# Attention and gated layer in one kernel: the two mask sizes read on one partition and spread by TensorE, fewer operations for the first masks, the later masks on GpSimd, and a new table of due dates

## The chip, the cores and the metric

One core of a Trainium2 chip runs the kernel. The metric is device time in microseconds (us). The kernel before takes 634.35 us, the median of 3 runs (634.06 to 634.65).

## The reference

Windowed attention with a few sink keys, followed by two dense layers with a gate between them. All inputs are float32; `n_sink` (4) and `window` (128) are two 64-bit integers that the kernel reads from memory while it runs.

```
q, k, v: (4, 8, 768, 64); w_in: (512, 2048); w_out: (2048, 512)
scores = (q @ k^T) / sqrt(64)
keep = (key < n_sink) | ((row - key >= 0) & (row - key < window))
a = softmax(where(keep, scores, -1e9)) / (sum + 1e-9)
x = (a @ v) as (3072, 512)
h = x @ w_in;  g = h - tanh(h);  out = g @ w_out
```

## The kernel before

**Work.** The 3072 rows are 12 chunks of 256 rows. Attention of a chunk is four units, one for each pair of heads. Unit u: its products (q times k, tile `s`) on TensorE, four merges on VectorE (add the mask, take the least, L727), four exponentials on ScalarE (L734), sums and reciprocals on VectorE (L742, L745), a scaling on GpSimd (L756) or ScalarE, transposes on TensorE (tile `t`), a copy on ScalarE (L766), and the products with the values (tile `x`). The dense layers of a chunk are eight groups of the hidden width: 24 matmuls `h` (L1023), a gate on ScalarE and VectorE, 12 matmuls `o` (L1075). The weights come as 64-bit words and are decoded on VectorE (L191 to L195).

**Order.** `Work.order` plans: every piece of work has an engine, a duration, a due date (which the table `PLAN` shifts) and its dependences. The planner takes the work in order of due dates as engines become free, and the result is each engine's program order. `BEGIN`, `COLD` and `came` are the planner's notions of when engines begin, until when TensorE is slow, and when the first keys and queries are there. Where the plan sees TensorE idle before its first dense step, `fill` puts in dummy matmuls of `ident` (tile `filled`, L1226). These are part of the program and run whether or not there is a gap.

**The start.** A first block stands ahead of the planned work: constants on GpSimd, the read of the sizes (`nswi`, L524) and of the first keys and queries, the masks of `_masks` on VectorE, and nine dummy matmuls (tile `warm`, L537). The two blocks are recorded separately and the framework puts them into one program per engine, so that an instruction of the second block can stand ahead of one of the first. Each engine runs its program in order.

**Masks.** The first chunks' units need `mask[:, 0]` (the diagonal block) and `wide` (two blocks side by side). Both depend on the sizes, which lie in `lim`. Three later closures (`merged`, `second`, `halves`, L159 to L175) make the masks of the later chunks and the row selectors `half` and `odd`, also on VectorE. The sizes reach all 128 partitions by one DMA that reads the same 16 bytes 128 times:

```
nc.scalar.dma_start(nswi, nsw.partition_broadcast(P))
```

The queries of units 0 and 1 follow it on ScalarE's DMA queue; unit 0's products need the queries and keys alone, the merges need products and masks. The products of units 0 and 2 share one pair of PSUM banks, those of 1 and 3 another, so that unit 2's products wait for unit 0's four merges.

Of the kernel before, what the change touches and what calls it, by code (L numbers as in the profile page):

```python
# [9 lines left out]
F32 = mybir.dt.float32  # L10
# [8 lines left out]
P = 128  # L19
# [4 lines left out]
NSK = 4  # L24
# [12 lines left out]
BIG = 3.0e38  # L37

# [4 lines left out]
    "first": -22200, "gate high": 12100, "gate low": -800, "gate tanh": 200, "second": -1800, "x high": -1700,  # L43
    "x low": 10100, ("attend", 0, 0): -2400, ("attend", 0, 2): 1300, ("attend", 2, 0): 1200, ("bits", 0): 26100,
# [3 lines left out]
    ("inverse", 1): 900, ("inverse", 2): -7600, ("late", 10, "values"): -7000, ("late", 11, "values"): 11500,  # L48
    ("late", 12): -5300, ("late", 13): -2400, ("late", 14): -200, ("late", 15): 8600, ("late", 16): -4400,
    ("late", 17): -2000, ("late", 18): 3600, ("late", 19): 1800, ("late", 20): -900, ("late", 22): -500,  # L50
    ("late", 23): -200, ("late", 24): 300, ("late", 25): 2900, ("late", 27): 2700, ("late", 28): -1900,
    ("late", 29): 3200, ("late", 30): 18900, ("late", 31): 500, ("late", 32): -8700, ("late", 34): 12800,
    ("late", 35): -2700, ("late", 36): -2000, ("late", 37): -2000, ("late", 38): -1200, ("late", 4, "values"): -8200,
    ("late", 40): -7200, ("late", 41): 100, ("late", 42): 12300, ("late", 43): -6000, ("late", 44): -500,
    ("late", 45): -11100, ("late", 46): 100, ("late", 47): 3800, ("late", 5, "values"): 1900,
    ("late", 6, "values"): 200, ("late", 7, "values"): -2200, ("late", 8, "values"): -4000,
    ("late", 9, "values"): 600, ("load", 10): -100, ("load", 2): -2100, ("load", 3): 3200, ("load", 4): -3200,
    ("load", 5): -500, ("load", 6): -200, ("load", 7): 8000, ("load", 8): 400, ("masks", 0): 5600,
    ("masks", 1): -2600, ("merge0", 0): 8900, ("merge0", 1): 5000, ("merge0", 2): -500, ("merge1", 0): 2600,
    ("merge1", 1): -3800, ("products", 0): 9800, ("products", 1): 1200, ("products", 2): -6300, ("scale0", 2): -500,  # L60
    ("step", 0): 18000, ("step", 1): 20100, ("step", 11): -1600, ("step", 12): 2900, ("step", 13): 100,
    ("step", 16): 3800, ("step", 17): -3300, ("step", 18): 600, ("step", 19): -700, ("step", 20): -300,
    ("step", 21): 600, ("step", 23): -3600, ("step", 25): -700, ("step", 26): -3400, ("step", 27): -1300,
    ("step", 28): 600, ("step", 29): -1600, ("step", 3): 100, ("step", 30): 2800, ("step", 32): -4500,
    ("step", 33): 600, ("step", 34): 500, ("step", 35): -4000, ("step", 36): -6600, ("step", 37): 100,
    ("step", 38): 4900, ("step", 39): 1200, ("step", 4): 800, ("step", 40): 5200, ("step", 41): -1200,
    ("step", 42): -5100, ("step", 43): 2900, ("step", 44): -1900, ("step", 45): 4400, ("step", 46): -3200,
    ("step", 47): -3300, ("step", 48): -1900, ("step", 49): 1000, ("step", 5): -900, ("step", 50): 3400,
    ("step", 51): 1200, ("step", 52): -1200, ("step", 53): -2300, ("step", 54): 6900, ("step", 57): -2900,
    ("step", 58): -2400, ("step", 59): -200, ("step", 6): 2800, ("step", 60): -6700, ("step", 61): -4300,  # L70
    ("step", 62): -200, ("step", 63): 700, ("step", 64): 500, ("step", 65): 7400, ("step", 66): 7000,
    ("step", 67): -1300, ("step", 69): -6600, ("step", 7): 900, ("step", 71): 1300, ("step", 72): 5100,
    ("step", 73): -100, ("step", 75): 2100, ("step", 76): -7500, ("step", 77): 400, ("step", 78): -13200,
    ("step", 79): 300, ("step", 8): -300, ("step", 80): -5700, ("step", 81): 1100, ("step", 84): 1600,
    ("step", 85): 1000, ("step", 86): -2400, ("step", 88): 1800, ("step", 9): -2000, ("step", 90): 14900,
    ("step", 91): -200, ("step", 92): 1000, ("step", 93): 3400, ("step", 94): 800, ("step", 95): -2000,
    ("sums", 0): -1000, ("sums", 1): -5200, ("sums", 2): -2200, ("transposes0", 0): 3600, ("transposes0", 1): -400,
    ("transposes0", 2): -3200, ("unit", 0): -100, ("unit", 1): 10700, ("unit", 10): -3200, ("unit", 11): 900,
    ("unit", 2): -1700, ("unit", 4): -3200, ("unit", 5): 1300, ("unit", 6): -8400, ("unit", 7): 1200,
    ("unit", 8): -2500, ("unit", 9): 4700, ("value in", 0): 2500, ("value in", 1): -1400, ("values", 0): 300,  # L80
    ("values", 1): -4700, ("values", 2): 7300, ("values", 3): 1400, ("values in", 1): -800, ("values in", 2): -4500,
    ("weights", 0, 0): -1800, ("weights", 0, 1): 1700, ("weights", 0, 2): 7300, ("weights", 0, 3): 11300,
    ("weights", 0, 4): 400, ("weights", 0, 5): 3700, ("weights", 0, 6): 700, ("weights", 0, 7): 8800,
    ("weights", 1, 0): 100, ("weights", 1, 2): -100, ("weights", 1, 3): -500, ("weights", 1, 4): 100,
    ("weights", 1, 5): -3900, ("words", 0, 0): 300, ("words", 0, 1): -5100, ("words", 0, 2): -100,
    ("words", 0, 3): -2200, ("words", 0, 5): 700, ("words", 0, 6): -200, ("words", 0, 7): 9400,
    ("words", 1, 0): 17700, ("words", 1, 1): 5500, ("words", 1, 2): 2100, ("words", 1, 3): 1300,
    ("words", 1, 4): 2700, ("words", 1, 5): -900, ("words", 1, 6): 700, ("words", 1, 7): 7400,
# [3 lines left out]
SCALES = (("POOL", "POOL", "ACT"), ("POOL", "POOL", "ACT"))  # L92
# [3 lines left out]
def kernel(  # L96
# [16 lines left out]
    nswi = cpool.tile([P, 4], I32, tag="nswi", name="nswi")  # L113

    pts = cpool.tile([P, NPAIR, 2, 4, P], F32, tag="pt", name="pt")
    et = mybir.EngineType
    bad = _banded(tc, cpool, qd, kp, vp, vs, nsw, nswi, w_in, w_out, ident, pts, out)


    with tc.If(bad != 0, preferred_fallthrough_block=True, label="rare"):  # L120
        _general(tc, qd, kp, vp, nswi, w_in, w_out, ident, xd, out)
# [1330 lines left out]
```

## Time and profile before

| | us |
|---|---|
| median of 3 runs | 634.35 |
| the profiled execution | 634.26 |
| its span on the engines | 632.5 |
| TensorE busy | 626.3 |
| VectorE busy | 365.7 |
| ScalarE busy | 303.7 |
| GpSimd busy | 51.5 |

The profiled execution lies within the three runs, and 1.8 us of it are outside the span. Busy time of TensorE holds its dummy matmuls too (`warm` and `filled`), so that a busy TensorE at the start need not be one that gets on. PE is TensorE's matmuls, PEld its weight loads, DVE VectorE, ACT ScalarE, POOL GpSimd; a q behind a name is the engine's queue of DMA issues. A float32 matmul shows as two records.

### The profile page before, as it was taken

To read this page: it belongs to the slowest core of one execution; us is meant where nothing else is said; L and a number is where in the kernel's file an instruction comes from. 1 tells how busy PE (TensorE), PEld (TensorE's weight loads), DVE (VectorE), ACT (ScalarE), POOL (GpSimd) and SP (SyncE) were. 2 spreads that over 40 slices of the span, in tenths; PEclk is the share of its full clock that TensorE was granted. 3 is DMA by queue.
4 is the path that set the end of the run, shared out by engine and by line. 5 is a ranking of instruction groups with operands and counts; after the bars stand their busy time and mean duration, and the time that the engine had idled before them with its cause. 6 is when DMAs were issued, how large, how long until landed. Compare 5 with 4: busy or idle time off the path is not lost.

```text
span 632.5 us, 14875 instructions
## 1 busy us (share of the span) xinstructions
PE 626.3 (99%) x5796; PEld 562.7 (89%) x5796; DVE 365.7 (58%) x1038; ACT 303.7 (48%) x851; POOL 51.5 (8%) x153
## 2 busy tenths in 40 slices
PE   9999999999999999999999999999999999999997
PEld 7788899989899899899989989999989899899995
DVE  8999999627556665346451655556562456632221
ACT  6857654337365464345352626547352445522222
POOL 4711010001000000000000000000000000000000
PEclk9999999999999999999999999999999999999999
DMA  8986242014343253133240125235332134210001
GB/s 259 365 345 205 89 139 66 1 67 136 105 160 106 72 169 118 32 117 113 61 148 34 52 77 175 78 80 172 106 97 72 51 85 137 96 30 2 33 1 37
DMA packets 70156, 67.81 MB, mean 107 GB/s; under 512 B 20929, under 2 KB 57537, under 8 KB 70081
## 3 DMA queue, kind: packets, MB, share of 16 engines
q1 hardware_dynamic: 69648, 66.55, 33.0%
q8 instruction: 47, 0.77, 0.5%
q10 hardware_dynamic: 432, 0.26, 0.2%
q14 instruction: 29, 0.23, 0.1%
HBM read 49.87 MB, written 16.91 MB: 106 GB/s over the span
## 4 chain that ended last, share of the span: by engine, by line
PE 99%; ACT 0%; issue 0%; DVE 0%; DVEq 0%; ACTq 0%
PE h L1023 42%; PE o L1075 42%; PE x L950 4%; PE s L620 3%; PE x L810 1%; PE t L762 1%; PE filled L1226 1%; PE s L716 1%; PE s_x L620 1%; PE warm L537 1%; PE x L938 1%; PE s_t L716 1%; ACT w L995 0%; ACT pt L766 0%; PE s_t L620 0%
## 5 line engine op out<-in xcount | busy, mean ns | idle before, releaser
L1023 PE MATMUL h<-xh,w 128*128 128x256 f32 x1536 | 277.9, 278 | 0.0
L1023 PEld LDWEIGHTS h<-xh,w 128*128 128x128 f32 x1536 | 237.6, 188 | 4.3 <-issue 1.2
L1023 PE MATMUL h<-xl,w 128*128 128x256 f32 x768 | 212.4, 277 | 0.0
L1075 PE MATMUL o<-w,gh 128*128 128x512 f32 x768 | 193.8, 392 | 0.0
L1075 PEld LDWEIGHTS o<-w,gh 128*128 128x128 f32 x768 | 139.2, 188 | 27.2 <-issue 0.8
L1031 DVE TENSOR_TENSOR h<-h,graw 128x512 f32<-128x512 f32 x96 | 66.8, 696 | 158.2 <-ACT graw L1028 157.7
L1023 PEld LDWEIGHTS h<-xl,w 128*128 128x128 f32 x768 | 144.3, 188 | 2.3
L1028 ACT ACTIVATE graw<-h 128x512 f32<-128x512 f32 x96 | 57.1, 595 | 161.2 <-PE h L1023 160.4
L1075 PE MATMUL o<-w,gl 128*128 128x512 f32 x384 | 103.5, 390 | 0.0
L1035 ACT CAST gh<-h 128x512 fp32r<-128x512 f32 x96 | 56.1, 585 | 64.6 <-DVE h L1031 49.8
L1039 DVE TENSOR_TENSOR gl<-h,gh 128x512 fp32r<-128x512 f32 x96 | 65.8, 686 | 35.3 <-ACT gh L1035 31.7
L1075 PEld LDWEIGHTS o<-w,gl 128*128 128x128 f32 x384 | 71.4, 188 | 14.8 <-issue 0.3
L648 ACT ACTIVATE p<-p,st 128x132 f32<-128x132 f32 x144 | 56.8, 397 | 31.4 <-DVE st L640 30.1
L672 ACT ACTIVATE p<-p,st 128x132 f32<-128x132 f32 x144 | 46.2, 397 | 4.2 <-DVE st L667 3.7
L864 DVE STREAM_TRANSPOSE pt<-p 128x512 f32<-128x512 f32 x36 | 25.5, 709 | 25.0 <-ACT p L672 25.0
L677 POOL CAST z<-p 128x16 fp32r<-128x16 f32 x36 | 7.1, 197 | 379.4 <-ACT p L672 305.1
L635 DVE COPY_PREDICATED s<-ident,s 128x256 f32<-128x256 uint32 x49 | 20.8, 425 | 15.7 <-PE s L620 15.2
L640 DVE CUSTOM_DVE_ANT_0 p<-s,mask 128x132 f32<-128x132 f32 x104 | 26.6, 293 | 2.6
L648 ACT ACTIVATION_READ_ACCUMULATOR p<-p,st 128x1 f32 x144 | 27.2, 189 | 0.0
L620 PEld LDWEIGHTS s<-kraw,qraw 64*64 64x64 f32 x832 | 21.8, 132 | 5.1 <-issue 3.9
L950 PE MATMUL x<-pt,v 64*64 64x192 f32 (+2 forms) x832 | 25.2, 271 | 0.0
L620 PE MATMUL s<-kraw,qraw 64*64 64x64 f32 (+3 forms) x832 | 24.6, 251 | 0.2 <-PE x L950 0.2
(109 smaller groups left out, 498.2 us busy)
## 6 DMA issues: line engine op xcount, KB each, us to landing
turned<-pt SPq DMA_DIRECT2D x36, 256.0 KB, 2.1
pt<-turned SPq DMA_DIRECT2D x144, 64.0 KB, 2.0
wraw<-w_in SPq DMA_DIRECT2D x16, 512.0 KB, 6.1
wraw<-w_out SPq DMA_DIRECT2D x16, 512.0 KB, 6.9
kraw<-kp SPq DMA_DIRECT2D x36, 196.0 KB, 3.1
out<-ob SPq DMA_DIRECT2D x24, 256.0 KB, 2.2
v<-vp SPq DMA_DIRECT2D x42, 128.0 KB, 2.9
qraw<-qd SPq DMA_DIRECT2D x40, 128.0 KB, 2.5
```

The source lines that it names most:

```text
L620: nc.tensor.matmul(y, lhsT=qt[u][HALF[h], t * P + half * Q : t * P + half * Q + Q], rhs=k, start=True, stop=True,)
L640: nc.vector.tensor_tensor_reduce(out=pr[u][:, j, :], in0=where[0][h][:, TS * t : TS * t + TS], in1=mask[:, kind, :], scale=-0.125, scalar= ...
L648: nc.scalar.activation(e, e, AF.Exp, bias=st[u][:, j : j + 1], scale=-1.0, accum_out=st[u][:, 4 + j : 5 + j],)
L672: nc.scalar.activation(pr[u][:, j, :], pr[u][:, j, :], AF.Copy, scale=s[:, 8 + j : 9 + j])
L864: nc.vector.transpose(dst, pr[u][:, :, NSK:].rearrange("p n (b j) -> p n b j", j=32))
L950: nc.tensor.matmul(xps[key][r][h * 64 : h * 64 + 64, j, a:z], lhsT=vt[cc, i][HALF[r], y, hd : hd + D], rhs=weight_columns(j, y, blk)[HALF[ ...
L1023: nc.tensor.matmul(y, lhsT=w, rhs=x, start=r == 0, stop=r == 11)
L1028: nc.scalar.activation(gr[n], hps[n], AF.Tanh)
L1031: nc.vector.tensor_tensor(hps[n], hps[n], gr[n], op=ALU.subtract)
L1035: nc.scalar.copy(gh[n], hps[n])
L1039: nc.vector.tensor_tensor(gl[n], hps[n], gh[n].bitcast(F32), op=ALU.subtract)
L1075: nc.tensor.matmul(y, lhsT=(gh, gh, gl)[i][n][:, f, t * P : (t + 1) * P], rhs=w, start=first and not low and r == 0, stop=bool(last and lo ...
```

## The change

The sizes are read once, into one partition (`one`). VectorE converts them to two floats, TensorE multiplies them with a row of ones (`ones`), which spreads them over 128 partitions, and VectorE copies the result into `lim`. The function `got`, which does this, is called in the middle of `_masks`. Instead of nine dummy matmuls there are four before and three after it. After the sizes are known VectorE does four mask operations on 128x128 ahead of the first merge; before it did six, with six of the later masks' operations between them. The masks of the later chunks and the selectors go to GpSimd (two bit operations stay on VectorE). All due dates and some of the planner's constants are new; one scaling of the third chunk goes from ScalarE to GpSimd; the piecewise first matmul of a block (`H_PIECES`, `O_PIECES`), there before after some kinds of work, is now used after `<lambda>` too (the early transposes and value products) and is of another form after `values`. `_general`, which does not run with these sizes, reads the sizes for itself.

```diff
-    "first": -22200, "gate high": 12100, "gate low": -800, "gate tanh": 200, "second": -1800, "x high": -1700,
+    "first": -700, "gate difference": -14100, "gate high": -1200, "gate low": -700, "gate tanh": -200,
...
-SCALES = (("POOL", "POOL", "ACT"), ("POOL", "POOL", "ACT"))
+SCALES = (("POOL", "POOL", "POOL"), ("POOL", "POOL", "ACT"))
...
+    back = mask[:, 1, NSK:]
+    nc.gpsimd.memset(mask[:, 0, :NSK], NEG)
 
     def halves():
         for pair, bit in ((half, 16), (odd, 32)):
             part = scr[:, 3, bit : bit + 1].bitcast(I32)
             nc.vector.tensor_scalar(part, rows, bit, None, op0=ALU.bitwise_and)
-            nc.vector.tensor_copy(pair[:, 0:1], part)
-            nc.vector.tensor_scalar(pair[:, 1:2], pair[:, 0:1], 1.0, None, op0=ALU.is_ge)
-            nc.vector.tensor_scalar(pair[:, 0:1], pair[:, 0:1], 1.0, None, op0=ALU.is_lt)
+            nc.gpsimd.tensor_copy(pair[:, 0:1], part)
+            nc.gpsimd.tensor_scalar(pair[:, 1:2], pair[:, 0:1], 1.0, None, op0=ALU.is_ge)
+            nc.gpsimd.tensor_scalar(pair[:, 0:1], pair[:, 0:1], 1.0, None, op0=ALU.is_lt)
...
+    nc.vector.scalar_tensor_tensor(wide[:, 1, :], above, FAR, diff, op0=ALU.mult, op1=ALU.add)
+    nc.vector.tensor_scalar(wide[:, 0, :], diff, 0.0, FAR, op0=ALU.is_ge, op1=ALU.mult)
+    nc.vector.scalar_tensor_tensor(wide[:, 0, :], wide[:, 0, :], float(P), diff, op0=ALU.add, op1=ALU.add)
+    got(lim, halves)
+    n_sink, window = lim[:, 0:1], lim[:, 1:2]
+    nc.vector.tensor_scalar(col, col, n_sink, NEG, op0=ALU.is_ge, op1=ALU.mult)
+    nc.vector.scalar_tensor_tensor(mask[:, 0, NSK:], wide[:, 1, :], window, col, op0=ALU.is_ge, op1=ALU.mult)
+    nc.vector.scalar_tensor_tensor(wide[:, 0, :], wide[:, 0, :], window, col, op0=ALU.is_ge, op1=ALU.mult)
+    nc.vector.tensor_scalar(wide[:, 1, :], wide[:, 1, :], window, NEG, op0=ALU.is_ge, op1=ALU.mult)
+    on = nc.gpsimd
+    on.tensor_scalar(below, diff, 0.0, None, op0=ALU.is_le)
...
+    on.tensor_tensor(mask[:, 1, :NSK], tmp[:, :NSK], col[:, :NSK], op=ALU.add)
...
-    BEGIN = {"PE": 5000.0, "ACT": 3600.0, "DVE": 5300.0, "POOL": 3000.0, "SP": 1700.0}
+    BEGIN = {"PE": 4600.0, "ACT": 3600.0, "DVE": 4900.0, "POOL": 8000.0, "SP": 1700.0}
...
-            nc.scalar.dma_start(nswi, nsw.partition_broadcast(P))
+            nc.scalar.dma_start(one[:, :4], nsw)
...
+            def got(lim, meanwhile):
+                two = one[:, 4:6].bitcast(F32)
+                nc.vector.tensor_copy(two, one[:, 0:4].rearrange("o (v w) -> o v w", w=2)[:, :, 0])
+                meanwhile()
+                nc.tensor.matmul(warm[:, 1, 1, 0:2], lhsT=ones, rhs=two, start=True, stop=True)
+                nc.vector.tensor_copy(lim, warm[:, 1, 1, 0:2])
...
+            keep_warm(4)
+            mask, above, below, after, half, odd = _masks(nc, outer, got, scr, wide)
+            keep_warm(3)
...
-            for _ in range(9):
-                nc.tensor.matmul(warm, lhsT=hot, rhs=hot, start=True, stop=True)
```

TensorE's program at its start, before. `s_191`, `s_202`, `s_229` and `s_247` are the products of units 0 to 3, `t_0_277` and `t_1_292` the transposes of unit 0.

```order
L537 MATMUL warm<-pt 128x128 x9
L716 MATMUL s_191<-lent_6_121 128x128 x2
L716 MATMUL s_191<-lent_6_121 128x256 x2
L716 MATMUL s_202<-lent_6_121 128x128 x2
L716 MATMUL s_202<-lent_6_121 128x256 x2
L1226 MATMUL filled<-ident 128x128 x5
L716 MATMUL s_229<-lent_6_121 128x128 x2
L716 MATMUL s_229<-lent_6_121 128x256 x2
L716 MATMUL s_247<-lent_6_122 128x128 x2
L716 MATMUL s_247<-lent_6_122 128x256 x2
L1226 MATMUL filled<-ident 128x128 x7
L762 MATMUL t_0_277<-ident,lent_7_124 128x128 x2
```

The same place now, where `s_207`, `s_215` and `s_249` are the products of units 0 to 2 and L545 is the matmul that spreads the sizes:

```order
L550 MATMUL warm<-pt 128x128 x4
L732 MATMUL s_207<-lent_6_120 128x128 x2
L732 MATMUL s_207<-lent_6_120 128x256 x2
L732 MATMUL s_215<-lent_6_120 128x128 x2
L732 MATMUL s_215<-lent_6_120 128x256 x2
L1242 MATMUL filled<-ident 128x128 x4
L545 MATMUL warm<-one,ones 128x2
L1242 MATMUL filled<-ident 128x128 x2
L550 MATMUL warm<-pt 128x128 x3
L1242 MATMUL filled<-ident 128x128
L732 MATMUL s_249<-lent_6_120 128x128 x2
L732 MATMUL s_249<-lent_6_120 128x256 x2
```

L545 was recorded ahead of all of the planned work, and in the program it stands behind the products of units 0 and 1 and four dummies. In all there were 28 `filled` and 9 `warm` before, and there are 27 and 7 now; behind unit 0's first transposes stand 20 of the `filled` now, where 16 stood before.

VectorE's program ahead of the first merge, before, from the mask operation that follows the sizes' two conversions to the first merge (L727); `lent_7_124` holds `wide` among others, `lent_7_125` the scratch:

```order
L152 TENSOR_SCALAR lent_7_125<-lent_7_125,few 128x128
L153 TENSOR_TENSOR lent_7_124<-mask,lent_7_125 128x128 [waits DVE_49]
L161 COPY mask<-lent_7_125 128x4 [waits DVE_49]
L162 TENSOR_SCALAR lent_7_125<-mask,few 128x128
L154 TENSOR_TENSOR mask<-lent_7_124,lent_7_125 128x128 [waits DVE_49]
L155 TENSOR_TENSOR lent_7_124<-lent_7_124,mask 128x128
L165 COPY mask<-mask 128x128 [waits DVE_49]
L156 TENSOR_TENSOR lent_7_124<-lent_7_124,lent_7_125 128x128 [waits DVE_49]
L166 TENSOR_TENSOR lent_7_125<-lent_7_125 128x128
L167 TENSOR_TENSOR mask<-lent_7_125 128x4 [waits DVE_49]
L727 ISA lent_7_124<-s_191,mask 128x128 [waits PE_49,Pool_49]
```

The same place now, where L543 converts the two sizes, L546 copies what TensorE spread, and L743 is the first merge:

```order
L543 CAST one<-one 1x2 [waits DMAHW0_49]
L149 TENSOR_SCALAR lent_7_124<-lent_7_124 128x1 [waits Pool_49]
L149 TENSOR_SCALAR lent_7_124<-lent_7_124 128x1
L546 COPY few<-warm 128x2 [waits PE_49]
L162 TENSOR_SCALAR lent_7_124<-lent_7_124,few 128x128 [waits DVE_49]
L165 SCALAR_TENSOR_TENSOR mask<-lent_7_123,few,lent_7_124 128x128 [waits DVE_49]
L166 SCALAR_TENSOR_TENSOR lent_7_123<-lent_7_123,few,lent_7_124 128x128
L167 TENSOR_SCALAR lent_7_123<-lent_7_123,few 128x128 [waits DVE_49]
L743 ISA lent_7_123<-s_207,mask 128x128 [waits Pool_49]
```

The chain from the sizes to the first merge is shorter on VectorE, and it now goes through TensorE's program by way of the wait of L546.

## Rows read from the trace of the kernel before

**Rows 1.** The page's busy times: busy us, share of the span, instructions.

```profile
PE 626.3 (99%) x5796; PEld 562.7 (89%) x5796; DVE 365.7 (58%) x1038; ACT 303.7 (48%) x851; POOL 51.5 (8%) x153
```

**Rows 2.** Stretches of the span: length, busy us by engine, granted clock, DMA share, GB/s.

```profile
2.00:4.00 2.00, 2.00 (x11) 2.00 (x11) 0.82 (x3) 1.28 (x1) 0.91 (x6) 1.00 0.52 98
4.00:6.00 2.00, 2.00 (x15) 1.59 (x13) 1.57 (x11) 0.00 (x0) 0.23 (x1) 1.00 1.06 364
10.00:25.00 15.00, 15.00 (x135) 12.31 (x134) 14.72 (x59) 13.22 (x49) 11.62 (x10) 1.00 1.00 357
25.00:50.00 25.00, 24.82 (x188) 20.92 (x187) 24.76 (x48) 17.41 (x44) 6.77 (x6) 1.00 0.87 335
```

**Rows 3.** Waits of TensorE in the whole span: total, times, longest.

```profile
PE s L620 <- PE x L950: 0.2, 1, 0.2
PE x L810 <- ACT pt L766: 0.2, 1, 0.2
```

**Rows 4.** Timeline of TensorE's first 12 us: start, duration, [idle before].

```profile
1.15 3.92 PEld L537 LDWEIGHTS warm<-pt 128*128 128x128 f32 x18 [1.15 <-DVE pt L520]
5.29 1.69 PE L716 MATMUL s<-lent 64*128 64x128 f32 x16
6.03 0.55 PEld L716 LDWEIGHTS s<-lent 64*128 64x128 f32 x8 [0.21 <-issue]
6.91 1.19 PEld L1226 LDWEIGHTS filled<-ident 128*128 128x128 f32 x10 [0.33 <-issue]
8.22 1.81 PE L716 MATMUL s<-lent 64*128 64x128 f32 x16
9.97 1.64 PEld L1226 LDWEIGHTS filled<-ident 128*128 128x128 f32 x14 [0.33 <-issue]
11.63 0.38 PE L762 MATMUL t<-ident,lent 128*128 128x128 f32 x2
```

**Rows 5.** All of the tile `filled`: records, min/median/max ns, first and last start.

```profile
L1226 PE MATMUL filled<-ident x56: 275/275/377, 6.9 to 25.0; 128*128 128x128 f32 x56
```

**Rows 6.** DMA issues of the first 12 us: KB each, us from issue to landing.

```profile
lent<-qd ACTq DMA_DIRECT2D x2, 128.0 KB, 4.0
nswi<-nsw ACTq DMA_DIRECT2D x1, 2.0 KB, 3.6
```

**Rows 7.** The page's DMA issues of the whole span, queries.

```profile
qraw<-qd SPq DMA_DIRECT2D x40, 128.0 KB, 2.5
```

**Rows 8.** Timeline of all engines' first 11 us, ScalarE's DMA issue and VectorE.

```profile
1.26 0.93 ACTq L127 DMA_DIRECT2D lent<-qd  x2
4.43 0.15 DVE L148 CAST few<-nswi 128x1 f32<-128x1 int32 x1 [1.61 <-DMA nswi<-nsw]
4.70 0.28 DVE L151 TENSOR_SCALAR mask<-mask,few 128x128 f32<-128x128 f32 x1
4.89 0.28 DVE L152 TENSOR_SCALAR lent<-lent,few 128x128 f32<-128x128 f32 x1
6.75 0.29 DVE L727 CUSTOM_DVE_ANT_0 lent<-s,mask 128x128 f32<-128x128 f32 x1
7.86 0.29 DVE L727 CUSTOM_DVE_ANT_0 lent<-s,mask 128x128 f32<-128x128 f32 x1
8.97 0.15 DVE L172 TENSOR_SCALAR lent<-lent 128x1 int32<-128x1 int32 x1
10.23 0.15 DVE L742 TENSOR_REDUCE lent<-lent 128x4 f32<-128x8 f32 x1
```

**Rows 9.** The same timeline, ScalarE's exponentials and GpSimd's first scaling.

```profile
7.08 0.40 ACT L734 ACTIVATE lent<-lent 128x128 f32<-128x128 f32 x1 [3.58 <-DVE lent L727]
8.85 0.49 ACT L734 ACTIVATE lent<-lent 128x256 f32<-128x256 f32 x1
10.77 3.18 POOL L756 TENSOR_TENSOR lent<-lent 128x256 f32<-128x256 f32 x4 [5.70 <-DVE lent L727]
```

**Rows 10.** The chain that ended last, in order of time: start, duration, blocks of 48.

```profile
79.50 5.65 PE h L1023 x48
94.66 5.45 PE h L1023 x48
```

More of the change, by code (lines that the diff above doesn't have):

```diff
@@ L51 @@
[L51 to L65, printed above, removed]
@@ L76 @@
[L76 to L80, printed above, removed]
@@ L86 @@
[L86 to L88 removed]
+    "first": -700, "gate difference": -14100, "gate high": -1200, "gate low": -700, "gate tanh": -200,
+    "second": 33200, "weights low": -2000, "x high": 3000, ("attend", 0, 0): -7100, ("attend", 0, 2): -1400,
@@ new lines @@
+    ("load", 4): 3200, ("load", 5): -9200, ("load", 6): 900, ("load", 7): 400, ("load", 8): -200, ("load", 9): -100,
+    ("masks", 0): 800, ("masks", 2): 2600, ("merge0", 0): -6100, ("merge0", 1): -300, ("merge0", 2): 12400,
+    ("merge1", 0): 1700, ("merge1", 2): -12000, ("products", 0): 7600, ("products", 1): -2500, ("products", 2): 3300,
+    ("scale0", 0): -26200, ("scale0", 1): -4100, ("scale0", 2): 1200, ("scale1", 0): -3200, ("scale1", 2): -800,
+    ("step", 0): -600, ("step", 1): -1300, ("step", 10): -7200, ("step", 11): 5100, ("step", 12): -3400,
@@ L527, in _banded, with keep_warm @@
                 _load_pair(nc.scalar, qt[u], qd[0, 2 * u : 2 * u + 2, :, :CH])
-                work.came.update({r: (5050.0, 5300.0)[u] for r in slots(u)})
+                work.came.update({r: (4600.0, 4900.0)[u] for r in slots(u)})
             make_identity(nc, ident)
-            mask, above, below, after, rest, half, odd = _masks(nc, outer, nswi, scr, wide)
             nc.gpsimd.memset(stats, 1e-9)
-            nc.gpsimd.memset(mask[:, 0, :NSK], NEG)
+            def got(lim, meanwhile):
[4 more added lines that the diff above has]
+                nc.vector.tensor_copy(lim, warm[:, 1, 1, 0:2])
+            def keep_warm(n):
+                for _ in range(n):
+                    nc.tensor.matmul(warm[:, 0, 0, :], lhsT=hot, rhs=hot, start=True, stop=True)
+            keep_warm(4)
+            mask, above, below, after, half, odd = _masks(nc, outer, got, scr, wide)
+            keep_warm(3)
             nc.gpsimd.memset(zt.bitcast(F32), 0.0)
             nc.gpsimd.memset(vsink.bitcast(F32), 0.0)
-            warm = ps_t.tile([P, 2, 2, P], F32, tag="t", name="warm")[:, 0, 0, :]
-            for _ in range(9):
-                nc.tensor.matmul(warm, lhsT=hot, rhs=hot, start=True, stop=True)
-        for i, part in enumerate(rest):
-            work.add("DVE", (650, 600, 1320)[i], 45000, part, (), ["mask", "scratch"], tags=(("masks", i),))
         def corners():
@@ L1246, in _rare, with _general @@
     return bad
-def _general(tc, qd, kp, vp, nswi, w_in, w_out, ident, xd, out):
+def _general(tc, qd, kp, vp, nsw, w_in, w_out, ident, xd, out):
     nc = tc.nc
```

116 lines of the change are left out of this document (63 added, 53 removed), and 6 rows, old and new, of the table PLAN.

## The prediction

> **What bounds the kernel now.** I read the busy times first, then the stretches, then TensorE's waits, then the first 12 us row by row. TensorE is busy for 626.3 of 632.5 us [rows 1], and apart from its beginning it waits for two things, 0.2 us each [rows 3]. So the dense part is a stream of matmuls with no holes, and time can be won or lost in two ways only: in what TensorE does that nobody needs, and in how even the stream is. The unneeded part lies in the first 25 us: 1.15 us before its first instruction, nine `warm` matmuls up to about 5.1 us, and 28 `filled` (56 records) from 6.9 to 25.0 us [rows 4, 5]. A `filled` costs 1.19 / 5 = 0.24 us [rows 4], so all of them 6.7 us. They hide a second bound. From 10 to 25 us VectorE is busy for 14.72 of 15 us, and from 25 to 50 us for 24.76 of 25 [rows 2]: the start goes at the pace of VectorE, and TensorE's dummies lie in its gaps.
>
> What starts VectorE's real work is the first merge at 6.75 us [rows 8]. The sizes land at 4.43 us; some 2.3 us of mask work follow. Unit 0's products start at 5.29 us [rows 4], right behind the landing of its queries (issue at 1.26 us and 4.0 us of flight give 5.26) [rows 6, 8], and are done before the masks. So the masks hold the first merge by a little, and the queries stand close behind.
>
> **The change, part by part.** The order of TensorE's program decides. The matmul that spreads the sizes stands behind the products of units 0 and 1 and four `filled`; every mask that VectorE still has to make, and so every merge, waits for it. Queued behind L546 on VectorE is everything it does; ScalarE waits for the merges, GpSimd and TensorE for ScalarE. I follow this chain and then add up TensorE's time.
>
> *Start of unit 0's products.* The 128 small reads are gone from the queue ahead of the queries. While they ran DMA moved 98 GB/s from 2 to 4 us, and 364 GB/s from 4 to 6 us, after they had landed [rows 2, 6]. The best that the queries could do is the flight of later ones, 2.5 us [rows 7]: 1.26 + 2.5 = 3.8 us. The worst is no change, 5.3 us. I take 4.7 us, a little above the middle, since keys and queries of two units still share the engines: **-0.6 us**.
>
> *TensorE's clock.* Before, 18 records of `warm` take 3.92 us, 218 ns each, and the same shape as `filled` takes 119 ns [rows 4]. That is the slow level (1.2 GHz) against the fast one (2.4 GHz), though the column of the granted clock says 1.00 for both [rows 2]; I go by the pace. The fast pace came after 3.9 us without a pause. Now four `warm` end at 1.15 + 8 x 0.218 = 2.9 us, and TensorE stands still until 4.7. Unit 0's products took 6.03 - 5.29 = 0.74 us [rows 4]; at the slow pace 0.74 x 218 / 119 = 1.36. I take one unit at the slow pace, **+0.6 us**. The bounds are none (0) and all until the sizes are spread (below).
>
> The Trainium skill, "TensorE: Matmul & The Clock Gate", Part 1: The HAM clock gate, says that the array's clock is throttled by default and that sustained activity releases it. The first rows agree in direction (218 ns, then 119); no row shows what a pause does. By that rule the shorter run of `warm` does not count and the slow pace lasts longer; that is the first rival.
>
> *To the first merge.* Unit 0: 4.7 to 6.1. Unit 1, with the gap behind it, 6.91 - 6.03 = 0.88 us [rows 4]: 7.0. Four `filled`: 7.9. L545 has no row; it costs between nothing and a lone transpose (0.38 us, [rows 4]). I take 0.3, since the weight load is the same however few columns follow: 8.2. Then VectorE: a hand-over of 0.1 (the exponential at 7.08 follows a merge of 0.29 begun at 6.75 by less than that [rows 8, 9]), the copy, and four mask operations at 0.2 to 0.25 us (4.70 to 4.89 is one step, [rows 8]; three-operand ones are unknown, hence the upper value), 1.2 us in all. The first merge is at 9.4 us, 2.65 us later than before, although the work behind the sizes shrank from 2.3 to 1.2 us.
>
> *From there to the transposes of unit 0.* Unit 0's merges take 7.86 - 6.75 = 1.1 us [rows 8], so unit 2's products can start at 10.6. TensorE, having done three `filled` and three `warm` (6 x 0.24), is there at 9.6: **idle 1.0**. Unit 3's wait for unit 1's merges, at 9.4 + 2.2 = 11.6 [rows 8]; products of two units take 9.97 - 8.22 = 1.75 us [rows 4], so **idle 0.2**, done at 12.5. Four exponentials take 1.8 us from 0.33 us behind the first merge [rows 8, 9]; with their tail and the second unit's merges VectorE comes to unit 0's sums at 11.7. Before it came to them at 10.23, 1.26 us after its last merge, because eight one-column operations of `halves` stood in between [rows 8]; these leave, and are worth 1.26 us on this chain. From the sums to the scaling are 0.54 us, and from there to the transposes 0.86 [rows 4, 8, 9]: 13.1 us, **idle 0.6**. Before: 11.63.
>
> *TensorE's sum.* Start -0.6, clock +0.6, L545 +0.3, three `warm` at the fast pace +0.7, one `filled` less -0.2, idle 1.0 + 0.2 + 0.6 = +1.8: +2.6 us. As a test, by the transposes: 13.1 - 11.63 = 1.5, and four more `filled` behind them 0.95 give 2.4. A lost microsecond can't be made good later, since the stream behind has no holes [rows 3].
>
> *The dense part.* A block of 48 `h` took 5.45 us, or 5.65 when it ran unevenly [rows 10]; the new pieces after early transposes and value products can spare some 0.1 us for 24 matmuls at four to seven places. I take **-0.4 us** (0 to -0.8).
>
> *Hidden.* GpSimd's masks: it stood idle for 5.7 us before its first scaling at 10.77 [rows 9], and the six operations behind the sizes, at some 0.3 us (a scaling takes 3.18 / 4 = 0.8 us on two to four times the columns), end near 11.5 us, before the scaling at 12.2. Without that cover each microsecond more delays the transposes as much. The moved scaling of the third chunk lies where ScalarE and GpSimd have room (17.41 and 6.77 of 25 us, [rows 2]). `_general` does not run.
>
> Together +2.2 us. The profiled execution took 634.26 us, 0.1 under the median, so 636.5 us.
>
> **The rivals.** *The clock stays low until the sizes are spread.* For it: a pause of nearly 2 us that was not there. Against: `warm` still runs 1.7 us. Unit 1 costs 0.55 x 99 / 119 = 0.5 us more, four `filled` 4 x 0.2 = 0.8, L545 0.2: +1.5 us, 638.0 us.
>
> *The queries land at 3.8 us and the clock is fast for them.* The whole chain moves by 0.9 + 0.6 us: +0.7, 635.0 us. For it: the low DMA rate beside the small reads. Against: it needs both best cases.
>
> *TensorE doesn't hold up the sizes, and the kernel is faster.* If the spread is there by the time unit 0's products end (6.1 us), the first merge comes at about 6.3 us. The transposes then come at 6.3 + 3.7 = 10.0 instead of 11.63; with four more `filled` and the pieces -1.6 + 0.95 - 0.4 = -1.1, 633.2 us. It decides whether L545 executes before 5 us. For it: VectorE's 1.26 us saved on a stage that it bounds. Against: the place in the program, behind matmuls that wait for queries.
>
> **How the numbers follow.** Forecast 0.57 (635.5 to 637.4), low clock 0.16, early queries 0.16, faster 0.11. A change under 0.2% (1.3 us) is about what a measurement of this kernel can't tell from none, so slower is above 635.6: the forecast without its lowest part, and the low clock, 0.70. Same: the early queries and that lowest part, 0.19. Faster 0.11. The range of 8 in 10 leaves out the faster case and the far end where late queries (+0.6) and a low clock meet: 634.2 to 638.6.
>
> **What would show it.** First merge between 9 and 10 us, right behind L546, which waits for TensorE; L545 after 8 us; TensorE idle for about 1 us before unit 2's products; no new waits after 25 us. If L545 stands before 5 us or the first merge before 7, the step on the order is wrong; if the pace of unit 0's products is fast, the step on the clock; if GpSimd's masks end after 12.2 us, they are not hidden; if TensorE waits in the dense part, the due dates matter, which I counted at nothing.

## The result, and the profile after

The changed kernel takes 638.8 us (median of 4 runs, 638.4 to 639.6) against 634.5 us, a ratio of 1.007 with an interval of 1.0052 to 1.0087. It is slower by 4.3 us. The forecast had the sign and half of the size, and its range ended at 638.6 us. The profiled execution has a span of 637.1 us, 4.6 us more than before. TensorE's busy time, against [rows 1]:

```profile
PE 628.2 (99%) x5792; PEld 564.9 (89%) x5792; DVE 365.7 (57%) x1024; ACT 301.9 (47%) x843; POOL 61.2 (10%) x173
```

That is 1.9 us more of busy time for four instructions fewer, so some of them ran slower, and 2.7 us more in which TensorE stood still. The stretches, in the columns of [rows 2], say where:

```profile
2.00:4.00 2.00, 1.23 (x6) 0.93 (x5) 0.71 (x6) 1.28 (x1) 1.09 (x7) 1.00 0.91 256
4.00:6.00 2.00, 1.57 (x10) 1.48 (x12) 0.00 (x0) 0.00 (x0) 1.85 (x6) 1.00 1.00 333
6.00:8.00 2.00, 2.00 (x13) 1.35 (x10) 0.00 (x0) 0.00 (x0) 0.77 (x3) 1.00 0.81 200
...
10.00:25.00 15.00, 13.64 (x107) 11.28 (x108) 14.21 (x63) 12.15 (x48) 11.55 (x16) 1.00 1.01 376
25.00:50.00 25.00, 24.78 (x204) 20.11 (x203) 24.03 (x56) 18.29 (x52) 10.72 (x8) 1.00 0.59 230
```

VectorE does nothing at all from 4 to 8 us. From 25 to 50 us TensorE is as full as before, and behind that it has no new wait of more than 0.2 us, so the loss lies in the first 25 us. The waits (total, times, longest) have two rows of over a microsecond on TensorE that [rows 3] do not have, and one very long one on VectorE:

```profile
DVE few L546 <- PE warm L545: 7.2, 1, 7.2
...
PE s L732 <- DVE lent L743: 1.2, 1, 1.2
PE s L732 <- DMA lent<-qd: 1.2, 1, 1.2
```

TensorE's timeline (start, duration, [idle before]) beside [rows 4]:

```profile
1.15 2.08 PE L550 MATMUL warm<-pt 128*128 128x128 f32 x8 [1.15 <-DVE pt L526]
4.43 2.93 PE L732 MATMUL s<-lent 64*128 64x128 f32 x16 [1.20 <-DMA lent<-qd]
7.29 2.07 PE L1242 MATMUL filled<-ident 128*128 128x128 f32 x8
9.29 0.58 PE L545 MATMUL warm<-one,ones 1*128 1x2 f32 x2
9.81 1.22 PE L1242 MATMUL filled<-ident 128*128 128x128 f32 x4
10.82 1.49 PE L550 MATMUL warm<-pt 128*128 128x128 f32 x6
12.10 0.64 PE L1242 MATMUL filled<-ident 128*128 128x128 f32 x2
12.67 1.95 PE L732 MATMUL s<-lent 64*128 64x128 f32 x16
14.61 0.44 PE L778 MATMUL t<-ident,lent 128*128 128x128 f32 x2
...
16.11 1.73 PE L1242 MATMUL filled<-ident 128*128 128x128 f32 x14
...
21.00 0.61 PE L1242 MATMUL filled<-ident 128*128 128x128 f32 x4
22.86 0.93 PE L732 MATMUL s<-lent 64*128 64x128 f32 x8 [1.25 <-DVE lent L743]
```

Read three things here. The spread (L545) stands at 9.29 us, behind both units' products and four `filled`. Everything up to 12.1 us runs at half pace: both units' products take 7.29 - 4.43 = 2.86 us, where they took 6.91 - 5.29 = 1.62 [rows 4], and eight records of `filled` take 2.0 us, 250 ns each, where fourteen at 16.11 us take 17.67 - 16.11 = 1.56 us, 111 ns each. And at 22.86 us unit 5's products wait for a merge. VectorE's and GpSimd's rows of the same timeline:

```profile
2.48 0.15 DVE L543 CAST one<-one 1x2 f32<-1x2 int32 x1
...
9.91 0.16 DVE L546 COPY few<-warm 128x2 f32<-128x2 f32 x1 [7.17 <-PE warm L545]
...
10.73 0.84 POOL L176 TENSOR_SCALAR mask<-mask,few 128x128 f32<-128x128 f32 x1
...
11.20 0.28 DVE L743 CUSTOM_DVE_ANT_0 lent<-s,mask 128x128 f32<-128x128 f32 x1
...
13.42 0.16 DVE L758 TENSOR_REDUCE lent<-lent 128x4 f32<-128x8 f32 x1
...
13.95 3.36 POOL L772 TENSOR_TENSOR lent<-lent 128x256 f32<-128x256 f32 x4 [0.49 <-DVE lent L761]
...
19.49 1.95 DVE L198 SCALAR_TENSOR_TENSOR pt<-wraw,pt 128x1024 uint32<-128x1024 uint32 x1
...
21.36 0.28 DVE L743 CUSTOM_DVE_ANT_0 lent<-s,mask 128x128 f32<-128x128 f32 x1
```

The sizes are on the chip at 2.48 us, two microseconds sooner than before [rows 8], and VectorE gets them at 9.91 us. The first merge is at 11.20 us (before 6.75) and unit 0's transposes at 14.61 us (before 11.63). A sum by the transposes: they are 3.0 us later, four more `filled` behind them cost 0.95, and unit 5's products wait 1.25. That is 5.2 us; the spans differ by 4.6. The 0.6 us that come back I put down to the later pieces, by the remainder alone: no run has the pieces by themselves.

### The profile page after: what moved, and what is told of

It is laid out like the page before. It is cut to its first block, busy times and chain, and to the rows that moved or that the text cites. A ratio compares the mean times of both kernels' runs of the same rounds, so it can differ in the third digit from the quotient of the medians.

```text
span 637.1 us, 14872 instructions
## 1 busy us (share of the span) xinstructions
PE 628.2 (99%) x5792; PEld 564.9 (89%) x5792; DVE 365.7 (57%) x1024; ACT 301.9 (47%) x843; POOL 61.2 (10%) x173
## 4 chain that ended last, share of the span: by engine, by line
PE 93%; DMA 4%; DVE 2%; issue 0%; ACTq 0%; ACT 0%
PE o L1091 42%; PE h L1039 41%; PE x L966 4%; PE s L636 3%; DMA wraw<-w_in 2%; DMA wraw<-w_out 1%; PE s_x L636 1%; PE x L826 1%; PE x L954 1%; DMA lent<-qd 1%; PE s_t L732 1%; PE t L778 1%; DVE pt L196 0%; DVE pt L198 0%; DVE lent L743 0%; DVE w L1016 0%
```

## The experiments

"Pace" is how fast TensorE gets through its matmuls, "place" where the spread stands in TensorE's program. I use "old dates" for the table of due dates, the pieces, the scalings' engines and the planner's constants of before. "One block" means that the prologue is recorded in the same block as the planned work; TensorE then has the source's order, with the spread ahead of all products. The ratio of each run is to the kernel before beside it (medians 634.6 to 634.7).

### The pace and the place, each alone

**a1_warm9**, the change with nine warm-up products ahead:

```diff
-            keep_warm(4)
+            keep_warm(9)
```

> The changed kernel with nine dummy matmuls instead of four ahead of the first products, all else as in the changed kernel; the matmul that spreads the sizes keeps its place behind the products of units 0 and 1. Theory of two causes (a late spread, and a clock that stays low because TensorE paused after four dummies): TensorE is fast from the first products on, which start at about 5.3 us instead of 4.43; the spread executes at 8.2 to 8.5 instead of 9.3, the first merge at 9.5 to 9.9 instead of 11.2, and the total is 637.0 to 637.7 us. Rival, the clock does not matter (only the place of the spread does): the products start 0.9 us later and everything behind them too, 639.4 to 639.8 us.

638.26 us (1.0059, 1.0046 to 1.0073), 0.6 us above what was expected and 1.1 below the rival. TensorE no longer pauses ahead of the first products, and both units' products take 1.5 us. The spread is at 7.49 us, the first merge at 9.20, and TensorE idles 1.04 and 0.19 us before the next two units' products; the forecast's chain had 9.4, 1.0 and 0.2. The transposes come at 12.60 us, 2.0 earlier than in the change. By the medians only 0.5 us of this arrive. Unit 5's products wait 1.25 us as in the change, and this does not touch the lead: they start at 20.85 instead of 22.86 us. Set beside each other matmul by matmul, the two traces keep the 2.0 us up to 562 us. There one wait of value products for ScalarE's `zr`, which the change's trace does not have, takes about half; the profiled executions end 1.0 us apart.

```profile
562.24 0.73 PE L954 MATMUL x<-zr,vsink 128*128 128x512 f32 x2 [0.74 <-ACT zr L948]
```

So with the pace mended, and unit 0's transposes half a microsecond earlier than the forecast had them (13.1), the kernel still takes 3.6 us more than before: the pace alone does not explain the time.

**a2_one_block**, the change with the prologue in one block:

```diff
-        with tc.manual_schedule(engines={et.PE, et.SP, et.DVE, et.Activation, et.Pool}):
+        def prologue():
...
         with tc.manual_schedule(engines={et.PE, et.SP, et.DVE, et.Activation, et.Pool}):
+            prologue()
             for n in todo:
```

> The changed kernel with its first block recorded in the same block as the planned work, so that the framework keeps the order as written: four dummies, the spread of the sizes, three dummies, then the products of unit 0. Theory, the late spread is the main cause: the spread executes at about 3.2 us, the products start at 4.5 and are slow at first, the first merge comes at 6.0 to 6.4 us instead of 11.2, the transposes of unit 0 at 10.0 to 10.8 instead of 14.6; the total is 634.0 to 635.2 us. Rival, the new due dates and the masks on GpSimd are the cause: the first merge moves as said, but waits behind 10 us or a later wait take the gain back, and the total stays above 637 us.

636.09 us (1.0026, 1.0016 to 1.0035). The spread is at 3.15 us, as expected. The first merge, at 7.39, is a microsecond later than expected: it now waits 2.16 us for unit 0's products and not for the masks, and both units' products still take 2.8 us. The time lies between the two theories. The place alone is worth 2.7 us, and 1.5 us are left.

**b1_warm4**, the kernel before with four warm-up products instead of nine:

```diff
-            for _ in range(9):
+            for _ in range(4):
```

> The kernel before with four dummy matmuls instead of nine ahead of the first products, all else as before. Theory of the clock: TensorE pauses from 2.9 us to the landing of the queries, the products of units 0 and 1 and the five dummies behind them run at the slow pace (some 220 ns a record instead of 119), unit 2's products start at 9.7 to 10.3 us instead of 8.2, and the total is 635.8 to 637.0 us. Rival, a pause of 2.4 us does not cost the clock: the pace is fast from the first products on, and the total is 634.3 to 634.8 us.

636.32 us (1.0027, 1.0018 to 1.0036). With nothing else changed, four warm-up products and the pause of 2.06 us behind them make both units' products take 2.9 us and cost 1.7 us. This shows the second cause by itself, though not whether the shorter warm-up or the pause makes it.

### The due dates

**b2_new_dates**, the kernel before with the new dates, and **a3_old_dates**, **a4_block_old**, **a5_block_old_warm**, **a6_broadcast_old**, four forms of the changed prologue with the old dates (two blocks; one block; one block with five warm-up products and the spread in its own PSUM tile; the new masks with the sizes by one DMA and nine warm-up products). Each replaces `PLAN`, the pieces, `SCALES`, `BEGIN` and `COLD` as a whole.

> The kernel before, its masks, its reading of the sizes and its nine dummies kept, with the new table of due dates, the new planner constants, the new place of the scaling and the new pieces. Theory, the due dates are worth little in themselves: 633.8 to 635.4 us, with no wait of TensorE over 0.5 us behind 10 us. Rival, they carry a good part of the loss (weights are asked for later, and a wait for decoded weights shows near 40 us): 636 us or more.

> The changed kernel with the table of due dates, the scalings' engines, the pieces and the planner's constants of the kernel before; the prologue stays that of the change, and the spread still stands behind the products of units 0 and 1 and some `filled`. If the due dates cost nothing (the prediction's reckoning), the time stays at 638.3 to 639.3 us and unit 5's products still wait. If the new dates cost 1.3 to 2 us (16 instead of 20 `filled` behind unit 0's transposes, no wait of unit 5's products behind three decodes), the time is 636.5 to 637.5 us, with unit 0's transposes still at 14 to 15 us.

> The same old dates, and the prologue recorded in one block with the planned work, so that the spread stands ahead of the products of units 0 and 1. Spread at about 3.2 us, first merge at about 7.4 us, unit 0's transposes at 11.2 to 11.8 us as in the kernel before. If order and dates are the two large causes, 634.2 to 635.2 us, no different from the kernel before; the slow pace of TensorE after the pause is left in it. If the slow pace by itself costs 1.7 us as four warm-up products cost the kernel before, 635.5 to 636.5 us.

> As the run before it, with five warm-up products ahead of the spread instead of four, and the spread in a PSUM tile of its own, so that the three warm-up products behind it need not wait for VectorE's copy of the sizes. TensorE then works from 1.2 to the first product of unit 0 with hardly a pause. If the pause keeps the pace low, the products of units 0 and 1 run in 1.5 us instead of 2.8 and the time is 632.8 to 633.9 us, faster than the kernel before; unit 0's transposes at 10.8 to 11.4 us. If the pace falls in any case, 634.2 to 635.2 us with both units' products in 2.8 us.

> The changed kernel's shorter first masks and its later masks on GpSimd, but the sizes read into all 128 partitions by one DMA as before, nine warm-up products in a row, nothing spread by TensorE, and the old due dates. If the masks themselves give time back, the first merge comes 0.4 to 0.8 us earlier than in the kernel before and the time is 633.4 to 634.3 us. If the masks on GpSimd are late for their readers or the two copies of GpSimd and VectorE hinder each other, 634.6 us or more, with a wait of VectorE for GpSimd in the first 20 us.

644.25 us for b2, and 653.09, 647.84, 648.87 and 648.36 us for the four: all above what was expected, by 8 to 16 us. The tile `filled` in a4 (records, min/median/max ns, first and last start) shows most of the reason; [rows 5] had 56:

```profile
L1245 PE MATMUL filled<-ident x142: 275/275/377, 8.4 to 32.8; 128*128 128x128 f32 x142
```

The old table was fitted to a planner that had three mask steps on VectorE. Without these steps the order of the units changes and the planner puts 43 more fillers into the gaps that it reckons with, in all four forms; b2, with the new table and the three steps, has 27 more. These five say nothing on the prologue, and only this on the dates: neither table fits a list of steps other than its own. The next four runs are built to avoid that.

### The old order, word for word

Three empty entries in the planner stand where before had its mask steps:

```diff
+        for i in range(3):
+            work.add("DVE", (650, 600, 1320)[i], 45000, lambda: None, (), ["mask", "scratch"], tags=(("masks", i),))
```

Behind the prologue every engine then has the order of before, with its 56 `filled`.

**c3_entries_broadcast**, the new masks alone, with the sizes by one DMA and nine warm-up products:

> The short first masks and GpSimd's later masks alone: sizes by one DMA into 128 partitions and nine warm-up products as before, old dates with the three empty entries, TensorE's order word for word that of the kernel before. The sizes are there at 4.4 us as before; the first merge then comes some 0.8 us earlier than before (6.0 instead of 6.75 us), as four operations and not nine lie between. 633.5 to 634.3 us if the fillers behind the merge give it on to the transposes; 634.3 to 634.9 us if the exponents and GpSimd's scalings take it up.

634.67 us (1.0001, 0.9992 to 1.001). The first merge is at 6.29 us, earlier by 0.46. It now waits for unit 0's products and no longer for the masks, and nothing of the gain arrives:

```profile
6.29 0.29 DVE L739 CUSTOM_DVE_ANT_0 lent<-s,mask 128x128 f32<-128x128 f32 x1 [0.56 <-PE s L728]
...
9.72 3.18 POOL L768 TENSOR_TENSOR lent<-lent 128x256 f32<-128x256 f32 x4
...
9.86 1.83 PE L1238 MATMUL filled<-ident 128*128 128x128 f32 x14
```

GpSimd's scaling starts a microsecond earlier than before (9.72 against 10.77 us [rows 9]), but TensorE has seven `filled` to do until 11.53 us whatever happens.

**c1_entries**, one block with four warm-up products, the spread, and three more, as the source of the change has it:

> The prologue of the change, recorded in one block with the planned work (spread ahead of the products of units 0 and 1), with the due dates, pieces and constants of before, and three empty entries in the planner where before had its three mask steps: behind the prologue every engine's order is then that of the kernel before, with its 56 `filled`, and only the masks differ, which GpSimd makes. First merge at about 7.4 us, unit 0's transposes at 11.2 to 11.8 us, no wait of unit 5's products. If late spread and new dates are what cost, 634.0 to 635.3 us, the kernel before within 0.2%. If the slow pace of TensorE costs by itself what four warm-up products cost the kernel before, 635.8 to 636.5 us. If later masks on GpSimd are a cause that was not seen, over 636.5 us.

635.97 us (1.0019, 1.001 to 1.0028). The first merge is at 7.39 us as expected; unit 0's transposes, at 12.58, are later than expected. TensorE's timeline:

```profile
3.16 0.58 PE L548 MATMUL warm<-one,ones 1*128 1x2 f32 x2
3.99 1.65 PE L553 MATMUL warm<-pt 128*128 128x128 f32 x6 [0.25 <-DVE few L549]
5.57 2.60 PE L738 MATMUL s<-lent 64*128 64x128 f32 x16
8.10 1.38 PE L1248 MATMUL filled<-ident 128*128 128x128 f32 x10
```

**c2_entries_warm**, the same with five warm-up products ahead and the spread in its own PSUM tile:

```diff
-                nc.tensor.matmul(warm[:, 1, 1, 0:2], lhsT=ones, rhs=two, start=True, stop=True)
+                spread = ps_x.tile([P, 2, CH], F32, tag="x", name="spread")[:, 0, 0:2]
+                nc.tensor.matmul(spread, lhsT=ones, rhs=two, start=True, stop=True)
...
-            keep_warm(4)
+            keep_warm(5)
```

> As the run before it, with five warm-up products ahead of the spread, and the spread in a PSUM tile of its own, so that the three behind it wait for nothing. If TensorE works on to the products of units 0 and 1 and keeps its pace, these take 1.5 instead of 2.8 us, unit 0's transposes come at 10.5 to 11.2 us and the time is 632.8 to 634.0 us, faster than before. If the pace falls here too, as the run before it.

636.12 us (1.0017, 1.0008 to 1.0026). The pace is low here too: both units' products took 2.7 us in the profiled execution, though TensorE worked on to them. There are five and three warm-up products here, with 0.2 us of idle time and half a microsecond of the two-column spread between them, and not nine in a row; whether the break or the missing ninth keeps the pace low, no run separates. Two of its eleven runs took 634.3 and 634.4 us; no profile shows what differed in them.

**c4_entries_late**, as c1 but in two blocks, the spread behind the products and four `filled` as the change has it:

> As the first of these, but recorded in two parts as the changed kernel is, so that the spread stands behind the products of units 0 and 1 and four `filled`; everything else is the order of before. What the late spread costs by itself: unit 0's transposes at 14.0 to 14.8 us instead of 11.63 and, with the slow pace, 636.6 to 638.0 us. The rest up to the changed kernel's 638.8 is then the dates' (0.8 to 2.2). If the dates cost nothing, 638.3 us or more.

638.49 us (1.0057, 1.0044 to 1.0071), 0.5 us above the first range and 2.5 over c1. Not all of this is the place. In the profiled execution, at 640.6 us the longest of the five, unit 0's transposes come at 17.14 us, later than in the changed kernel (14.61), because the pace falls a second time: behind a wait of 1.39 us for unit 0's merges the products of units 2 and 3 take 14.91 - 12.22 = 2.69 us, and the granted clock from 14 to 16 us is 0.50.

```profile
12.22 2.76 PE L734 MATMUL s<-lent 64*128 64x128 f32 x16 [1.39 <-DVE lent L745]
14.91 2.39 PE L1244 MATMUL filled<-ident 128*128 128x128 f32 x14
```

```profile
14.00:16.00 2.00, 2.00 (x11) 1.35 (x10) 1.71 (x13) 2.00 (x11) 1.87 (x3) 0.50 0.74 251
```

The changed kernel's trace has no such second stretch, and whether the other four executions of c4 have it is not known. So neither the 0.3 us from here to the changed kernel nor the second theory's 638.3 us tells what the new dates cost; the pairs a2 and c1, and e1 and d2 below, do.

**d2_spread_after_warm**, c1 with nine warm-up products ahead of the spread and none behind it; **d1_late_warm9**, c4 with nine ahead:

```diff
-            keep_warm(4)
+            keep_warm(9)
...
-            keep_warm(3)
```

> One block, the order of before, nine warm-up products, then the spread and at once the products of units 0 and 1: TensorE spreads the sizes but at no point pauses. If the slow pace is the whole of the 1.3 us that the spread ahead of the products cost, both units' products take 1.5 to 1.7 us from 5.7 us on, unit 0's transposes come at 11.7 to 12.2 us and the time is 634.5 to 635.3 us, the kernel before within 0.2%. If the spread costs by itself or lowers the pace, 635.7 us or more.

> The changed prologue in two parts (spread behind the products of units 0 and 1 and four `filled`), the order of before behind it, and nine instead of four warm-up products ahead, so that TensorE goes from them to the products without a pause. It takes the slow pace away and leaves the late spread. If both cost about half, unit 0's products and the fillers run fast, the first merge comes at about 9.2 us, unit 0's transposes at 13.3 to 13.8 us instead of 17.1, and the time is 636.2 to 637.2 us (638.5 with four). If the pace is worth nothing, 638 us or more; if it is all, 635 us or less.

d2: 634.99 us (1.0003, 0.9995 to 1.0012). TensorE spreads the sizes, does not pause, and both units' products take 7.31 - 5.80 = 1.5 us:

```profile
1.15 4.21 PE L553 MATMUL warm<-pt 128*128 128x128 f32 x18 [1.15 <-DVE pt L530]
5.29 0.58 PE L548 MATMUL warm<-one,ones 1*128 1x2 f32 x2
5.80 1.58 PE L737 MATMUL s<-lent 64*128 64x128 f32 x16
7.31 1.38 PE L1247 MATMUL filled<-ident 128*128 128x128 f32 x10
```

So the 1.0 us between d2 and c1 is the pace (by the medians; the two profiled executions are 0.3 us apart), and the spread in an early place costs 0.4 us, which can't be told from nothing.

d1: 638.89 us (1.0058, 1.0041 to 1.0074), no better than c4. Its runs fall apart, 636.9, 637.1 and 638.1 us against 639.7 to 640.1, and the profiled one is of the upper kind; in it the granted clock falls after the wait of 1.4 us for unit 0's merges (stretches, columns of [rows 2]):

```profile
10.00:12.00 2.00, 0.91 (x8) 0.52 (x8) 2.00 (x15) 1.83 (x9) 1.92 (x7) 1.00 1.00 350
12.00:14.00 2.00, 1.81 (x13) 1.15 (x12) 1.65 (x13) 2.00 (x11) 1.52 (x3) 0.67 1.00 387
14.00:16.00 2.00, 2.00 (x11) 2.00 (x11) 1.26 (x9) 1.15 (x6) 1.81 (x3) 0.50 0.83 270
16.00:18.00 2.00, 2.00 (x20) 2.00 (x20) 0.43 (x3) 1.26 (x6) 0.00 (x0) 0.98 0.87 283
```

Fourteen records of `filled` behind that wait took 2.94 us, where they take 1.65. The lower two runs are within the expected 636.2 to 637.2; that the upper ones owe their 3 us to this second pause is shown for the profiled one alone, as in c4.

### What is left to gain, and the change repaired

**d3_fewer_fillers**, c3 with GpSimd's two clearings ahead of its masks and six `filled` fewer, and **b3_before_fewer**, the kernel before with the same six fewer:

```diff
+        for g, k in zip([n for n in todo if spare.get(n)], (0, 4, 1, 1)):
+            spare[g] = max(0, spare[g] - k)
```

> The short masks and GpSimd's masks with sizes by one DMA as before and nine warm-up products (634.7 us), with GpSimd's two clearings of `z` and `vsink` put ahead of its masks and six `filled` fewer around unit 0's transposes (3, 2 and 3 instead of 7, 3 and 4). If what the earlier masks give is only held back by fillers and GpSimd, unit 0's transposes come at 10.5 to 10.9 us instead of 11.5 and the time is 633.5 to 634.3 us, below before by 0.1 to 0.2%. If it is given back at a later wait, 634.4 to 635 us, with a wait of TensorE for GpSimd, ScalarE or VectorE in the first 25 us.

> The kernel before with the same six `filled` fewer, beside the run before this one. There the transposes of unit 0 start as the first scaling ends (10.77 us and 0.8 us behind), so that nothing is gained: 634.3 to 635.0 us, transposes at 11.5 to 11.7 us. If fillers by themselves hold the front back, 633.9 us or less.

634.41 us (0.9996, 0.9987 to 1.0005) and 634.40 us (0.9998, 0.9989 to 1.0006). In d3's trace unit 0's transposes come at 11.31 us, later than expected, and TensorE has waits in place of the fillers:

```profile
PE t L774 <- ACT pt L778: 0.6, 2, 0.3
PE t L774 <- DVE xl L847: 0.3, 1, 0.3
```

That trace is a poor witness, though. It is of the longest of eleven executions, 635.9 us, and in it the products of units 0 and 1 took 7.71 - 5.32 = 2.39 us in spite of nine warm-up products (b3's took 2.19):

```profile
5.32 2.46 PE L728 MATMUL s<-lent 64*128 64x128 f32 x16
7.71 1.38 PE L1240 MATMUL filled<-ident 128*128 128x128 f32 x10
```

So the earlier masks bring nothing that can be measured; that it is ScalarE and VectorE that take the gain is shown for this one execution only. No run here beats the kernel before by what can be measured.

**e1_repaired**, the whole change with its own new dates, in one block and with nine warm-up products ahead of the spread and none behind:

> The whole change with its own new due dates, repaired in both places: one block, so that the spread stands where the source has it, and nine warm-up products ahead of it and none behind, so that TensorE does not pause. If the dates cost nothing and place and pace are the two causes, 634.8 to 635.4 us, the kernel before within 0.2%, though unit 5's products still wait for VectorE's third decode. If the dates cost what that wait takes (1.2 to 1.5 us), 636 us or more.

635.07 us (1.0004, 0.9995 to 1.0013).

```profile
4.92 0.38 PE L549 MATMUL warm<-one,ones 1*128 1x2 f32 x2
5.23 1.70 PE L735 MATMUL s<-lent 64*128 64x128 f32 x16
...
10.49 0.44 PE L781 MATMUL t<-ident,lent 128*128 128x128 f32 x2
```

Unit 0's transposes come 1.1 us before those of the kernel before, and still nothing is won: four more `filled` (0.95) and 1.2 us of unit 5's wait stand behind them, and some 0.6 come back as in the change.

## Why the prediction was half right

| step | forecast | measured in the change | alone |
|---|---|---|---|
| the late spread holds up the first merge | 9.4 us | 11.20 us | +2.7 us (the change less a2), +3.2 (a1 less e1) |
| TensorE's slow pace | +0.6 us | all up to 12.1 us | +0.5 (the change less a1), +1.0 (c1 less d2, a2 less e1), +1.7 (b1) |
| due dates | 0 | a wait of 1.25 us | 0.1 (a2 less c1, e1 less d2) |
| masks on GpSimd | hidden | hidden | 0.0 (c3, with the shorter first masks) |

**The order** was right: the spread's place in TensorE's program holds up all merges, VectorE waits 7.2 us for it, and putting it right gives 2.7 to 3.2 us (the change to a2; a1 to e1, which also has three warm-up products fewer).

**Two steps failed**, and the sum by the transposes separates them. The forecast had them 1.5 us late, 0.95 us of `filled` behind them and -0.4 for the pieces, 2.05 us. Measured are 3.0, 0.95, a wait of 1.25 that the forecast does not have, and -0.6: 4.6 us. Some 1.5 us of the miss lie ahead of unit 0's transposes, and 1.25 behind them.

**The clock is the first step that failed**: "I take one unit at the slow pace, +0.6 us". The first merge came 1.8 us later than forecast. The queries gave 0.3 back (4.43 instead of 4.7 us); both units' products together took 2.86 instead of 2.3 us (+0.6), four `filled` 2.0 instead of 0.9 (+1.1), L545 0.52 instead of 0.3 (+0.2), and the way from it to the merge 1.4 instead of 1.2 (+0.2). That is nearly the first rival's chain, which had the pace low until the sizes are spread and the merge at 10.9 us; the three `warm` behind it were slow too, 1.28 instead of 0.7 us. The idle time that I forecast before unit 2's products is not in the trace because TensorE, slower, came there late itself: slow work took the place of idle time in the sum, and that the sum still gave half of the loss is partly luck. In a1, where TensorE is fast, both idle times are there to a tenth. The rival's 638.0 us is near the measured time, but it has no wait of unit 5's products in it either.

The Trainium skill, "TensorE: Matmul & The Clock Gate", HAM oscillation — how this bites in real kernels, describes a kernel whose bursts of matmuls are shorter than the waits between them, so that every burst starts on the slow clock again. b1, c1 and c2 are not that case, since the pace there had not risen yet (both units' products at 2.5 to 2.9 instead of 1.6 us); they agree with the default state that the prediction cited from the Trainium skill, and the rival that follows from it had 0.16. c4 and d1 come nearer: there the pace had risen and fell again, but behind a single wait of 1.4 us with more work than that ahead of it.

**The due dates are the second**, a term that was put at nothing: in the new order three decodes stand on VectorE ahead of unit 4's merges, the last at 19.49 us for 1.95 us, and unit 5's products wait 1.25 us for them. I had said that a lost microsecond can't be made good later and did not ask what else the new order makes late; my sign for it looked behind 25 us, and this wait stands at 22.86. Against the old dates under the same prologue the new ones as a whole cost nothing that can be measured (a2 and c1, e1 and d2), because they also bring unit 0's transposes forward, to 11.61 from 12.58 us and to 10.49 from 12.14, and give that back at the wait and at four more `filled`.

**Hidden work**: GpSimd's masks behind the sizes took up to 0.84 us each and not 0.3, and the last ended near 13 us instead of 11.5. They stayed hidden because VectorE's sums, at 13.42 us, were as late; my sign, an end after 12.2 us, came true and misled, since the scaling had moved back too.

**The rival on the faster side** was priced too well. It gave 633.2 us for an early spread at no loss of pace. e1 is that case, with the transposes at 10.49 us (the rival had 10.0), and takes 635.07 us, since the wait of unit 5's products, which the rival lacks too, takes the lead back.

What stays open: whether it is the shorter warm-up or the pause behind it that leaves the pace low; what the executions of c4 and d1 have that no profile shows; what the pieces are worth by themselves; and whether the wait for `zr` stands in a1's other executions.

## What to carry to other kernels

An operand that goes through an in-order engine arrives when that engine's program gets there: look at the compiled order, not at the source, before a broadcast is moved from a DMA queue to TensorE. A shorter warm-up is not a saving of its own length; price all work up to the next change of pace at the slow one. A table of due dates fits only the list of steps that it was made for, so to test a prologue alone keep the list, with empty entries if need be. And a lead at the start counts only if no later wait takes it: set the two traces beside each other along the whole span.

## What the hardware showed that I had not expected

TensorE kept the slow pace (213 ns and more for a record of `filled` or `warm`) from its first instruction to 12.1 us, with a pause of 1.2 us ahead of the first products, while the granted clock stood at 1.00 in every stretch; in c4 and d1 the same pace, behind a later pause, shows as 0.50. The column of the first microseconds is therefore no proof of the pace. The traces' records of the granted clock begin only where the pace rises, at 5.28 us before and at 13.47 us in the change; ahead of the first record a stretch shows 1.00.

That moment differs between executions. With nine warm-up products in a row the first record lies between 4.4 us (a1) and 7.2 (d3), and at 6.72 us in b3, whose TensorE program begins as that of the kernel before. A single trace is therefore no measure of what the pace costs; the medians are.

The sizes read into one partition could be used at 2.48 us, where VectorE did not have to wait for them, against 4.43 us for the read into 128 [rows 8]; the queries behind them came 0.9 us sooner (4.43 against 5.29).
